# A DeltaNet and hardswish-MLP kernel on one core: the hand-written order of its first steps rewritten, the order of the loads with it

## The chip, the cores and the metric

The kernel runs on one core of a Trainium2 chip. The metric is the device time of one execution in microseconds (us). Before the change the median of three runs is 661.89 us (661.52 to 662.9). The engines are PE (TensorE, matmuls), DVE (VectorE), ACT (ScalarE), POOL (GpSimd) and SP (SyncE, which here only issues loads and stores). Each runs its own instructions in the order in which they were written; a semaphore holds an instruction back until what it reads is there.

## The reference

```
B, H, S, D = 4, 8, 768, 48
k_n = k / (norm(k, axis=-1) + 1e-6)
for t in range(S):                      # a state of D x D for each batch and head
    y[t] = q[t] @ state
    v_old = state^T k_n[t]
    state = state + beta[t] * outer(k_n[t], v[t] - v_old)
x = y as (3072, 384)
h = x @ w_in                            # 384 x 2048
out = (h * clip(h + 3, 0, 6) / 6) @ w_out   # 2048 x 384
```

The two weight matrices come as 64-bit floats, and the kernel converts them to FP32 itself.

## The kernel before

The recurrence over 768 tokens is cut into 24 chunks of 32 tokens (chunk t), all four batches side by side on 128 partitions. Chunk t needs a unit lower triangular 32x32 matrix per batch and head to be inverted. Chunk 0 is inverted alone by block products (`product`). Chunks 1 to 4 form group 1: their sixteen-row halves are solved together on DVE by `halves_of(1)`, and `join(t)` makes one inverse out of two halves. From chunk 5 on four chunks are solved together by `inverse(g)`. Two chunks give 256 tokens for the MLP (a block); `up` is its first matmul, `down` the second. The 16 weight pieces of 768 KB (eight of w_in, eight of w_out) are loaded raw and converted by ACT (four steps, L345) and DVE (three steps, L367, L372, L378).

For chunks 0 to 4, while the weights arrive, the order is not computed but written out: `ORDER` is a string of 782 words, `word*n` meaning n times. `do(word)` advances one generator by one step, and a step issues its instructions on one engine. So the string fixes the order on every engine, SP's loads included. After the string ends, a planner takes over whose code is the same in both kernels.

What the words issue, in the order of their steps (a chunk number follows the letter):

| word | steps |
|---|---|
| k, q, v | one load of 48 KB on SP (a chunk is four); L168, L180, L193 |
| w, W | one weight piece on SP, L320; W waits for the last PE instruction written before it |
| B | one load of beta, issued by ACT, L1383 |
| z | on DVE: zero pads; transpose of beta (L247); `eye`, `blocks`; `corner`; nothing; `parity` (nine small fills, L265 and L268) |
| s | on POOL: pads, and the state's zeros |
| n0, n1, n2, n4, n5 | key norms: square (ACT L396), sum (DVE L402), root (ACT L406), three small DVE steps, `inv` (DVE L420) |
| p | kb (POOL L499), transpose of keys (PE L513), copy KQ (ACT L521), transpose of queries (PE), copy KQ (ACT), products sc (PE L536), L and LB (DVE L547) |
| m, b | mask times beta (POOL L475); beta times kb (POOL L487) |
| x0 | `product(0)`: 16 steps; PE at L585, DVE L595 to L645, two ACT copies V at L613 and L632 |
| i1 | `halves_of(1)`: transpose A (DVE L458), 28 DVE steps, a fill, transpose X (DVE L462) |
| x1 to x4 | `join`: fill (POOL), transpose (DVE L683), PE L673, two DVE steps (L687, L691), PE L673, copy X (ACT L699) |
| h | `chain`: ks (PE L795, not for chunk 0), R (DVE L890, L898), pz (PE L816), copy Z (ACT L916), su (PE L927), state (DVE L945) |
| y | output: even (ACT L832), odd (DVE L808), py (PE L816), sum or copy (L850, L852), yt (PE L862), copy xT (ACT L866); chunk 0 has the last four only |
| a, c | the ACT steps (four a piece) and DVE steps (three a piece) of the weights |
| ua, ra, ga (ub, ...; u, ...) | `up` of one half block, one 128-wide part each: PE L983, ACT L990, DVE L993; u are the MLP's later units |

In the texts, `a2.1` is piece 2's second ACT step, `c6.0` piece 6's first DVE step, `W2` piece 2's load, `ga4` the fifth ga, and so on.

A part of `up` holds one of four PSUM banks until its ga has read it, so the fifth part behind it waits for that ga. `needs` in the code is a check on the written order only and issues nothing.

## Time and profile before

| | |
|---|---|
| median of three runs | 661.89 us (661.52 to 662.9) |
| profiled execution | 662.71 us; its span from first to last instruction 661.0 us, so 1.7 us lie around it |
| PE busy | 632.6 us of the span (96%) |
| DVE busy | 499.5 us (76%) |
| ACT busy | 263.2 us (40%) |
| POOL busy | 226.6 us (34%) |
| mean granted PE clock | 0.989 |
| DMA | 33.28 MB |

The page has a row for each engine in which a digit is the busy share of one fortieth of the span (16.5 us) in tenths. The view by windows gives busy microseconds of each engine in a stretch. The timeline lists the instructions of an engine with their start, duration and the idle time before them, with what ended it. The chain of waits follows the end of the run back from instruction to instruction.

### The profile page before, as it was taken

The page shows a single profiled execution, that of the slowest core. Times are in us where ns is not written, and L with a number is a line of the kernel's source. Part 1 is how long each engine was busy: PE and PEld are TensorE (multiplying, and loading weights), DVE is VectorE, ACT ScalarE, POOL GpSimd, SP SyncE. Part 2 cuts the span into 40 slices and gives each one's busy share as a digit, 9 for nine tenths or more (in the row PEclk, how much of TensorE's full clock was granted, in tenths as well). Part 3 has the DMA queues.
Part 4 walks back from the last instruction along what each step waited for, and adds up shares of the span by engine and source line. Part 5 has one row for each costly group of instructions (what it writes and reads, how often), then busy time and mean ns, then how long its engine had stood idle before and what let it go on. Part 6 is the DMA issues. An engine that isn't in the chain of part 4 may idle for free.

```text
span 661.0 us, 26631 instructions
## 1 busy us (share of the span) xinstructions
PE 632.6 (96%) x11640; PEld 568.8 (86%) x11640; DVE 499.5 (76%) x1164; ACT 263.2 (40%) x547; POOL 226.6 (34%) x352
## 2 busy tenths in 40 slices
PE   2768999999999999999999999999999999999997
PEld 2658987776689989999999999999999999999997
DVE  5899877798657988758988748979658998456354
ACT  4786578322232154154144244244244144153240
POOL 5531023003661354453254354164152241331330
PEclk9979999999999999999999999999999999999999
DMA  7888246212041030041030030030020020000101
GB/s 171 210 216 217 76 100 165 49 25 39 16 84 20 2 75 3 3 83 28 3 74 3 2 74 3 2 63 2 3 50 2 2 49 3 23 18 2 26 1 24
DMA packets 88692, 33.28 MB, mean 50 GB/s; under 512 B 80224, under 2 KB 83424, under 8 KB 88576
## 3 DMA queue, kind: packets, MB, share of 16 engines
q1 hardware_dynamic: 88224, 31.29, 21.5%
q8 instruction: 91, 1.49, 0.9%
q10 hardware_dynamic: 352, 0.30, 0.2%
q14 instruction: 25, 0.20, 0.1%
HBM read 26.84 MB, written 4.72 MB: 48 GB/s over the span
## 4 chain that ended last, share of the span: by engine, by line
PE 91%; DVE 3%; DMA 2%; ACT 2%; SPq 1%; issue 1%; ACTq 0%; DVEq 0%
PE po L1215 28%; PE ph L1055 27%; PE ph L983 9%; PE po L1151 6%; PE ks L795 4%; PE pz L816 3%; PE pt L513 3%; PE py L816 3%; PE su L927 3%; PE sc L536 3%; ACT spare L345 1%; PE yt L862 1%; DMA w_out<-in_moe_w_in_dram 1%; SPq L168 1%; PE pi L673 1%
## 5 line engine op out<-in xcount | busy, mean ns | idle before, releaser
L1055 PE MATMUL ph<-xT,w_in 128*128 128x128 f32 (+1 forms) x720 | 156.7, 321 | 0.2 <-issue 0.2
L1019 POOL TENSOR_TENSOR g<-g 128x256 f32<-128x256 f32 (+1 forms) x144 | 88.0, 612 | 105.5 <-ACT g L1069 99.9
L1055 PEld LDWEIGHTS ph<-xT,w_in 128*128 128x128 f32 x720 | 116.9, 191 | 6.7
L1215 PE MATMUL po<-w_out,g 128*128 128x192 f32 x640 | 110.6, 326 | 0.0
L1215 PEld LDWEIGHTS po<-w_out,g 128*128 128x128 f32 x640 | 104.6, 190 | 0.5
L1215 PE MATMUL po<-spare,g 128*128 128x192 f32 x480 | 86.7, 332 | 0.0
L1069 ACT ACTIVATE g<-ph 128x512 f32<-128x512 f32 x72 | 43.0, 597 | 107.5 <-PE ph L1055 107.5
L1215 PEld LDWEIGHTS po<-spare,g 128*128 128x128 f32 x480 | 77.2, 190 | 1.8
L983 PE MATMUL ph<-xT,w_in 128*128 128x128 f32 (+1 forms) x384 | 72.8, 339 | 1.5 <-ACT xT L866 0.6
L1225 POOL TENSOR_TENSOR o<-o,u 128x192 f32<-128x192 f32 x18 | 14.9, 828 | 163.5 <-ACT o L1222 76.1
L983 PEld LDWEIGHTS ph<-xT,w_in 128*128 128x128 f32 x384 | 60.2, 196 | 9.0 <-DVE g L993 0.9
L1082 DVE TENSOR_TENSOR g<-ph,g 128x256 f32<-128x256 f32 x72 | 30.2, 419 | 47.3 <-PE ph L1055 44.8
L748 DVE TENSOR_TENSOR pr<-A 128x30 f32<-128x30 f32 (+9 forms) x150 | 57.6, 384 | 3.3
L1201 DVE TENSOR_TENSOR g<-g 128x512 f32<-128x512 f32 x80 | 55.3, 712 | 3.6 <-PE po L1215 3.6
L1102 DVE SCALAR_TENSOR_TENSOR g<-o,g 128x512 f32<-128x512 f32 x72 | 52.5, 729 | 7.2 <-ACT o L1099 7.2
L753 DVE TENSOR_TENSOR A<-A,pr 128x30 f32<-128x30 f32 (+9 forms) x150 | 55.1, 367 | 3.3
L1055 PE MATMUL ph<-beta_tok,sums_in 128*128 128x128 f32 x288 | 55.9, 275 | 0.1
L1099 ACT ACTIVATE o<-g 128x512 f32<-128x512 f32 x72 | 45.4, 631 | 12.0 <-DVE g L1102 8.5
L345 ACT ACTIVATE spare<-spare 128x768 uint16<-128x768 uint16 (+1 forms) x56 | 47.3, 850 | 3.2 <-DMA kf<-in_k_dram 1.7
L499 POOL TENSOR_TENSOR kb<-kf,inv 128x384 f32<-128x384 f32 x24 | 21.7, 906 | 75.5 <-issue 42.6
L1222 ACT ACTIVATE o<-po 128x192 f32<-128x192 f32 x40 | 13.2, 330 | 83.2 <-PE po L1215 83.2
L1151 PE MATMUL po<-w_out,g 128*128 128x384 f32 x128 | 45.4, 490 | 0.0
(137 smaller groups left out, 1010.2 us busy)
## 6 DMA issues: line engine op xcount, KB each, us to landing
kf<-in_k_dram SPq DMA_DIRECT2D x96, 48.0 KB, 3.0
qb<-in_q_dram SPq DMA_DIRECT2D x96, 48.0 KB, 2.6
vf<-in_v_dram SPq DMA_DIRECT2D x96, 48.0 KB, 2.5
out_dram<-o SPq DMA_DIRECT2D x90, 48.0 KB, 1.6
spare<-in_moe_w_in_dram SPq DMA_DIRECT2D x4, 768.0 KB, 5.3
w_out<-in_moe_w_in_dram SPq DMA_DIRECT2D x4, 768.0 KB, 5.6
w_out<-in_moe_w_out_dram SPq DMA_DIRECT2D x4, 768.0 KB, 7.0
spare<-in_moe_w_out_dram SPq DMA_DIRECT2D x4, 768.0 KB, 4.9
```

Source lines behind the costliest of these rows:

```text
L345: nc.scalar.activation(out=z, in_=z if n else d.bitcast(I16)[:, :, :, 3], func=func, bias=value, scale=scale,)
L748: nc.vector.tensor_tensor(out=pv, in0=A[:, j + 1 :, j].unsqueeze(2).to_broadcast([n, w, j]), in1=A[:, j, 0:j].unsqueeze(1).to_broadcast([n ...
L753: nc.vector.tensor_tensor(out=A[:, j + 1 :, 0:j], in0=A[:, j + 1 :, 0:j], in1=pv, op=ALU.subtract)
L983: nc.tensor.matmul(ph[:, cols], lhsT=w_in[:, s, f * 128 : (f + 1) * 128], rhs=xT[:, s, cols], start=(s == 0), stop=(s == NKT - 1),)
L1019: nc.gpsimd.tensor_tensor(out=out, in0=a, in1=b, op=op)
L1055: nc.tensor.matmul(ph[:, n], lhsT=w, rhs=x, start=start, stop=stop, skip_group_check=True)
L1069: nc.scalar.activation(out=gt, in_=ph[:], func=ACTF.Copy)
L1099: nc.scalar.activation(out=r, in_=g, func=ACTF.Relu, bias=0.5, scale=1.0 / 6.0)
L1102: nc.vector.scalar_tensor_tensor(out=g, in0=r, scalar=1.0, in1=g, op0=ALU.min, op1=ALU.mult)
L1151: nc.tensor.matmul(pos[c][:], lhsT=gs[blk, f // 2][:, f % 2, c * P : (c + 1) * P], rhs=w_out[:, f, :], start=(f == 0), stop=(f == NFC - 1),)
L1201: nc.vector.tensor_tensor(out=A(f, *out, 4), in0=A(f, *a, 4), in1=A(f, *b, 4), op=op)
L1215: nc.tensor.matmul(ps[n][:], lhsT=A(f - f % 2, *a)[:, f % 2], rhs=b[:, f], start=(f == 0), stop=(f == HF - 1),)
```

## The change

The string holds the same 782 words, each as often as before, in another sequence. Its last 29 words stand as they did. Three checks on the order are added in the code, and none of them issues an instruction. On SP the first weight pieces now come after fewer key and query loads:

| piece | k and q loads ahead, before | after |
|---|---|---|
| W0 | 8 and 4 | 8 and 4 |
| W1 | 14 and 4 | 12 and 4 |
| W2 | 18 and 6 | 17 and 6 |
| W3 | 20 and 10 | 19 and 10 |
| W4 | 22 and 15 | 21 and 14 |
| W5 | 23 and 18 | 21 and 16 |
| W6 | 24 and 23 | 21 and 20 |
| W7 | 28 and 23 | 26 and 23 |

The start of the string, as far as the end of `halves_of(1)`, and the code:

```diff
 ORDER = """
-k*2 B*3 k*2 n0 k*2 z B s*2 n0*6 k*2 q*2 n1 q n1 q w k p0 z*3 k n1*2 k*2 n1*2 z p0*2 s k p0*3 a k a
-m0 a n2 m1 p0 x0*2 w q x0 n1 x0*3 c*2 n2 a k s p1*2 a s*2 k q s*2 x0 n2 k*2 c x0 n2 x0 w q a*4 q p1
-n2 k*2 a x0 m2 p1 c*2 p1 n2*3 b1 q b0 s p1 x0 q w x0 n2 q*2 c*3 x0 n4 k p1 k p2*2 x0*2 a*2 c a*2 q*3
-a*2 w v p3*2 q x0 q n4 p2*2 c p2 v c n4*2 a*3 z v n4 c a m3 v c p2 n4*2 q p2 k c b2 h0 c h0 w a*2 h0
-p4*2 a*2 m4 p3 q*4 h0 q k w p4*2 c*5 v*2 p3 k p3*3 k*2 p4*2 v*2 p4 m6 k a w a w i1*3 k i1*7 a i1*2 a
-i1*2 v i1*2 k b3 k y0 c y0*3 ua*2 ra*2 i1*3 w v ga v a*3 i1*2 ua i1 h1 i1 q w ua ra ua i1 ra*2 ga i1
-k ua a*2 ra ga i1 ga ua ra ua ra i1 ga i1*4 ua ga n5 x1*2 k x1 c a ra v a*2 ga x2 k*2 ga*2 ua*2 x1
...
+k*3 B*2 k n0*2 k n0 k*3 s n0*3 n1 q n1 q*2 n1 q w k*2 n0 p0 B*2 z k n1 z k m0 p0 n1 p0 n1 w s z p0*3
+a p0 x0*2 s x0*2 n1 x0 a c k p1 c s n2 x0 n2 q a s a p1 a q x0 s c k*2 s k n2*2 s x0 k x0 w q a n2*2
+a k a c s b1 x0 p1 n2 x0 z n2 a c q k q x0 p1 b0 c m1 q w p1*2 n2 x0 a k*2 m2 z c q c x0 q p2 p1 x0
+a*3 n4 a q c n4 a q a w p2 q c a n4 p2*2 v x0 p2 c n4 v n4 c q p3 b2 c a p3 v n4 a n4 p2 v a m3 c p3
+w h0 p2 p3 h0 a h0 p4 a q*2 c q a*2 p3 q h0 c*2 w p4 k c p4*2 c v q k p4 k p3*2 c m4 p4*2 y0 v k i1
+k a q m6 i1 v q w i1 q a i1 w i1 y0 a*2 i1*3 y0*2 ua*2 i1 v i1 a v*2 i1*3 c i1*3 b3 ua w k*2 ra a i1
+k ga ra a k i1 k i1 ga ra i1 ua i1 z ua i1 ga v ua ra n5 h1 i1 ga i1 a ra i1*3 a ua ra ua i1 w i1*2
+ga ra y1 k i1 ua x2 x1 ga x1 a k ga v x1 ra a n5 x1 k n5 ga k ra ua ga ua x1*2 ra h1 ga v ua ra a c
...
@@ settings
         pads(nc.vector, kbufs[0], qbufs[0])
+        past.add("first pads")
         yield
+        needs(*(("B", b) for b in range(B)))
         nc.vector.transpose(out=beta_tok[:].rearrange("p n h -> p (n h)"), in_=beta_hm)
@@ prep
+        needs("first pads")
         for j, src in enumerate((kb, qb)):
@@ chain
-        needs(("bkb", t))
+        needs(("bkb", t), ("state", t - 1))
         su = update() if t < N - 1 else []
@@ betas
             nc.scalar.dma_start(out=beta_hm[C * b : C * b + H, :], in_=beta[b])
+            past.add(("B", b))
             yield
```

Engine by engine, the moves that matter here read so:

| engine | before | after |
|---|---|---|
| ACT, beta's loads | three ahead of the first square, the fourth behind it | two ahead, two behind chunk 1's root |
| DVE, first norms | stt2 of chunk 0, inv, sum of chunk 1, transpose of beta | stt2 of chunk 0, sum of chunk 1, inv, pads, ..., transpose of beta |
| ACT, first copy V of x0 | a0.0, a0.1, a0.2, square, V | a0.0, V, a0.1, square, a0.2 |
| ACT, second copy V of x0 | a1.3, a2.0, KQ of chunk 1's keys, root, a2.1, KQ of its queries, V | root, a1.2, a1.3, KQ of chunk 1's keys, V, a2.0, KQ of its queries, a2.1 |
| PE, around x0's last products | sc of chunk 1, x0, kb transpose of chunk 2, x0 | sc of chunk 1, x0, x0, both transposes of chunk 2 |
| ACT, end of the first chunks | a5.3, KQ of chunk 3's keys, 4's keys, 3's and 4's queries, a6.0 to a6.3, y0 | KQ of chunk 3's keys, Z0, a5.0 to a5.3, KQ of 3's queries, 4's keys and queries, a6.0, a6.1, y0 |
| DVE, parity | between chunk 4's norm steps | between the 21st and the 22nd step of i1 |
| PE, first ups | three ua, ks of chunk 1, six ua, join | six ua, ks of chunk 1, three ua, join |
| SP, piece 12 (W) | behind the second ub | behind the tenth ub |

More of the change, by code (lines that the diff above doesn't have):

```diff
@@ L28 @@
-i1*2 v i1*2 k b3 k y0 c y0*3 ua*2 ra*2 i1*3 w v ga v a*3 i1*2 ua i1 h1 i1 q w ua ra ua i1 ra*2 ga i1
-k ua a*2 ra ga i1 ga ua ra ua ra i1 ga i1*4 ua ga n5 x1*2 k x1 c a ra v a*2 ga x2 k*2 ga*2 ua*2 x1
-ra*2 x1*2 ua h1*2 n5 k ga c ra ga*2 h1 c y1*2 ua ra w ga ua ra x2 n5 ga y1*2 ua ra ga h1 v*3 n5*2 k
-y1*2 ua a ra x2 ub*2 a n5 rb*2 h1 x3 ga c*2 v W a h2 y2 gb ub rb gb x2 gb ub*2 n5*2 b4 rb n5 x2*2 h2
-gb rb gb m5 a n5*2 y2 ub rb gb v c q*2 v q*5 n5 ub n5 rb gb h2 c h2 q ub y2 h2 y2 rb ub p5 b5 rb
@@ L33 @@
-gb*2 a*2 x3 p5 ub y2*2 k p5*2 h2 rb h3 p5 gb h3 ub*2 q rb gb rb gb ub a x3 p6 v c x4 x3 rb gb ub p7
-rb gb y3 c*2 v c p7*2 y3 v p7*2 b6 x3 q x3 ub p6 h3 a p6 c p5*2 rb gb k m7 w p6 h3 u p6 k*2 q*3 a*2
-y3 a p6 c y3 v y3*2 u n9 v k q a c a c*2 u*2 ru gu w k a*2 c a*2 x4 c*2 ru p7 a gu k u a*2 p7 p6 m8
-u*3 a k u*2 k h3 w ru*2 a*2 gu*2 x4 c*2 x4 k c*2 a p8 k a*2 u ru k h3 u*2 h4 ru a b8 gu k gu y4 p8*3
-u h4 k*2 c q k*9 q u p8*2 x4 k ru k*2 gu k c n9 q u q*2 p8 k*2 b7 n9*2 i2 u x4 q i2*2 q ub ru gu u
@@ L38 @@
-rb gb i2*2 h4*2 u*2 i2 ru i2*6 y4 i2 gu i2*7 u i2 ru gu i2 u*3 ru i2*4 gu ru i2*2 v i2 c gu u*3 a u
-ru c i2 u*2 i2 gu i2*3 q i2*5 y4 h4 n9 i2 e*2 n9*2 i2*4 q i2 y4 e n9 u ru i2*3 u i2 ru*2 gu h4 u n9
-i2*2 u i2 e i2*6 y4 u k n9*3 u gu i2 y4 n9 i2 p9 q i2*2 gu
+k*3 B*2 k n0*2 k n0 k*3 s n0*3 n1 q n1 q*2 n1 q w k*2 n0 p0 B*2 z k n1 z k m0 p0 n1 p0 n1 w s z p0*3
+a p0 x0*2 s x0*2 n1 x0 a c k p1 c s n2 x0 n2 q a s a p1 a q x0 s c k*2 s k n2*2 s x0 k x0 w q a n2*2
+a k a c s b1 x0 p1 n2 x0 z n2 a c q k q x0 p1 b0 c m1 q w p1*2 n2 x0 a k*2 m2 z c q c x0 q p2 p1 x0
@@ new lines @@
+ra ga c ua h1 c h1 y1 ua ra a ga y1 k ra h1 n5 y1 x2 ga ua ra ga y1*2 ua ra q x2 v ub ga rb ub c a
+rb c h1 ga h2 n5 w x2 ub k gb rb gb q n5 h2 gb ub q v rb x3 x2 v ub x2 rb ub b4 n5 gb rb gb v n5 ub
+n5 gb c q h2 n5 y2 rb q h2 ub q y2 n5 c n5*2 ub y2 h2 y2 gb y2 rb ub rb a q gb a*2 rb p5 gb b5 a W k
+x3 gb p5 ub y2 h2 v rb ub v p5 v a h3 p5 q a gb k p7 x3 k rb ub m5 h3 gb y3 k ub p5 p6 v x3 rb c p7
+gb v rb gb ub b6 c y3 c p7 x3 p7 x3 p6 p7 c h3 a p6 v p5*2 h3 p7 rb w a p6 m7 q u p6 y3 k c y3 c x4
@@ new lines @@
+k p6 a k y3 u gb y3 q u a*3 k q a c u c u ru k gu k ru n9 c*2 u p6 p7 a*2 gu w a k u*2 w a p8 ru*2 c
+a x4 c k m8 a q k gu k q c u a u c x4 gu k h3 c k x4 u h3 a k ru q u gu ru b8 gu p8 a k p8 q c h4 p8
+h4 a y4 u*3 k*2 a q p8*2 k a k n9 x4 ru k*3 gu k u c q*2 p8 n9*2 i2 u x4 q i2 q i2 k q ub ru gu u rb
+gb i2*2 h4*2 u*2 i2 ru c i2*2 b7 i2*3 y4 i2 gu i2*7 u i2 ru gu i2 u*3 k ru i2*5 gu ru i2*2 v i2 c gu
+u*3 a u ru c i2 u*2 i2 gu i2*3 q i2*5 y4 h4 n9 i2 e*2 n9*2 i2*4 q i2 y4 e n9 u ru i2*3 u i2 ru*2 gu
@@ L41 @@
+h4 u k*2 n9 i2*2 u i2 e i2*6 y4 u k n9*3 u gu i2 y4 n9 i2 p9 q i2*2 gu
 """
```

## The prediction

> **What bounds the kernel now.** I read the page's slices first, then the view by windows, then the chain of waits, then the timelines of ACT and DVE.

> ```profile
> PE   2768999999999999999999999999999999999997
> DVE  5899877798657988758988748979658998456354
> ACT  4786578322232154154144244244244144153240
> PEclk9979999999999999999999999999999999999999
> ```

> PE is full from the fifth slice (66 us) to the end, and what follows the string is the same code. So the change is worth what it moves the moment from which PE is full, plus what it does to PE's few gaps behind that. The windows cut that start into stages (columns: PE, PEld, DVE, ACT, POOL busy us, granted clock, DMA share, GB/s):

> ```profile
> 31.00:36.00 5.00, 4.27 (x156) 3.55 (x160) 4.24 (x17) 2.48 (x5) 1.96 (x2) 0.60 0.88 217
> 36.00:40.00 4.00, 2.71 (x126) 2.44 (x115) 3.83 (x8) 3.90 (x6) 2.57 (x3) 0.50 0.63 116
> 40.00:46.70 6.70, 4.94 (x204) 4.23 (x202) 6.47 (x13) 6.43 (x11) 0.83 (x1) 0.84 0.86 185
> 46.70:59.70 13.00, 10.26 (x121) 9.29 (x121) 12.21 (x40) 8.33 (x18) 2.26 (x5) 0.87 0.98 280
> 59.70:71.00 11.30, 10.20 (x367) 9.15 (x368) 9.74 (x27) 6.40 (x17) 2.14 (x4) 1.00 0.35 95
> 71.00:83.00 12.00, 12.00 (x442) 11.22 (x442) 9.94 (x28) 7.08 (x19) 1.83 (x2) 1.00 0.40 101
> ```

> From 36 to 59.7 us DVE is the full engine (3.83 of 4.00, 6.47 of 6.70, 12.21 of 13.00, where its steps on group 1 follow each other without a gap longer than 0.1). From 71 PE is. The handover is in the chain (start, length, what):

> ```profile
> 46.75 1.88 DVE A L458
> ...
> 57.67 1.99 DVE X L462
> 59.78 0.37 DVE sums_in L683
> 60.19 0.73 PE pi L673 x54
> ```

> DVE transposes group 1's matrices (L458, at 46.67 in the timeline), solves, transposes back (L462), and the first join's transpose (L683, 59.69) lets PE start its product at 60.19. By then PE has done the same nine `ua` and one ks in both orders, with 0.57 and 0.92 us of idle time just ahead. So PE has room there, and **the start of L683 is the moment to be forecast**.

> Where DVE still waits, ahead of 46.67, the timelines say (start, length, what, idle before and its end). ACT:

> ```profile
> 15.18 0.51 ACT L396 ACTIVATE sq<-kf 128x384 f32<-128x384 f32 x1
> 15.59 0.36 ACT L613 ACTIVATE sums_in<-pi 128x256 f32<-128x256 f32 x1
> ...
> 22.46 0.93 ACT L345 ACTIVATE spare<-w_out 128x768 uint16<-128x768 int16 x1 [0.42 <-DMA w_out<-in_moe_w_in_dram]
> ...
> 25.09 0.38 ACT L632 ACTIVATE sums_in<-pi 128x256 f32<-128x256 f32 x1
> ```

> and DVE:

> ```profile
> 7.11 0.20 DVE L420 RECIPROCAL inv<-nt 128x8 f32<-128x8 f32 x1
> 7.36 0.55 DVE L402 TENSOR_REDUCE ss<-sq 128x8 f32<-128x384 f32 x1
> ...
> 25.50 0.45 DVE L634 STREAM_TRANSPOSE sums_in<-pi 128x256 f32<-128x256 f32 x1 [0.82 <-ACT sums_in L632]
> ...
> 40.28 1.01 DVE L945 TENSOR_TENSOR state<-state,su 128x384 f32<-128x384 f32 x2
> ```

> **The change, part by part.** All 782 words stay, so no engine gains or loses work; only waits change. I walk DVE's new sequence with the durations of the old rows.

> 1. *First norms.* `inv` of chunk 0 (7.11) goes behind chunk 1's sum (7.36), into the place that the transpose of beta had at 7.83. POOL's kb started 0.29 behind `inv`, at 7.40, so now at 8.12, and with it its transposes, KQ and sc: the first L moves from 12.25 to 12.97, a loss of 0.72.

> 2. *Beta.* Its last load started at 5.10, and the DMA view shows that queue's last packets between 6.5 and 7.0, so it takes at most 1.9. Now two loads follow chunk 1's root (7.94 to 8.15), at about 0.4 each: the last starts at 8.55 and has landed by 10.45. Transpose 0.97 and POOL's mask 1.19 make 12.6, ahead of 12.97. Hidden by 0.35; without that cover it costs what it overruns.

> 3. *First V of x0.* It ran at 15.59, behind two ACT steps of W0 and a square, though PE was done at 14.95. Now only a0.0 is ahead of it, which waits for W0 (SP's issue 7.49, landed 12.56, same place in SP's queue) and ends at 13.5. PE ends at 14.95 + 0.72 = 15.67, V starts at 15.7 and DVE's transpose at 16.1 instead of 15.99. Of 0.72 only 0.1 is left.

> 4. *Second V of x0.* It ran at 25.09, behind a2.0 (22.46, which had waited for W2), a KQ, a root and a2.1; DVE stood still for 0.82 and, for that root, 0.53. Now it stands ahead of all of piece 2. PE's product, at 22.19 to 23.27, gets the 0.1; ACT reaches V at about 23.85 (a1.2, a1.3 and one KQ behind the root at 21.4), DVE is free at 24.45 and transposes there: 1.05 early. One wait is new: PE's next product of x0 stands behind sc of chunk 1, whose second KQ is now behind a2.0, so it ends at 28.7 and DVE goes on at 28.75 against 30.09; one c step that stood ahead follows now. At c3.1 DVE is 0.96 early (32.45 against 33.41).

> 5. *The weight pieces.* W1 to W6 lose one to five loads ahead of them, at 0.45 to 0.49 each on SP; W5 went out at 31.93 and by the same sum goes out near 28.5. Before, ACT waits once for a piece at 0.42 (22.46) and once for PE at 2.49 (33.88). I value earlier pieces by themselves at nothing: ACT is full from 24 us in the new order (24 steps of 0.85 and the KQ until 43), and no piece is late for it. If they gave all they could, it would be that 0.42. W12 goes out later, behind the tenth `ub` (82 us) instead of at 73.3; its first reader on ACT is at 99, and a piece lands in 4.5 to 8.4.

> 6. *State of chunk 0.* DVE's step at 40.28 follows su (38.43 to 39.73). New: sc of chunk 2 at 34.4 (34.53), pz 1.50, Z at 37.4, where ACT ends a4.3 and a KQ (37.90), su at 38.0 to 39.3. DVE, free at 38.3, waits for it a microsecond and goes on at 39.35: still 0.93 early. Then three steps of piece 5 and c6.0, L of chunk 3, c6.1, L of chunk 4 (KQ's end at 43.1, sc at 44.2, both in time): 6.4 us as before, so L458 at 45.75 against 46.67, **0.92 early**. This also counts that parity (34.75 to 35.27, 0.52) has left this stretch.

> 7. *Parity* now lies between two steps of the solve: 0.5 more from L458 to L683, otherwise the same 13.02 (28 steps, both transposes, c6.2, ga0 to ga5). `ua` starts near 47.8 instead of 48.99 and PE's room ahead of the join grows; no gain comes of that, as the join still stands behind nine `ua`. L683: 59.69 - 0.92 + 0.5 = 59.27, **0.42 early**.

> 8. *Behind it*, from 60.19 to 70.99 (the second join's product), PE idles 0.31 and 0.30. The new sequence sends su of chunk 1 ahead of a `ua`, and puts the sum of chunk 1's output (DVE, due 9.2 us behind L683) just ahead of PE's need. I count 0.55 back; nothing or the full 0.61 are the ends.

> Sum: 0.42 + 0.55 = 0.97, so about **1.0 us less**: 661.7 for the profiled execution (662.71, of which 1.7 lies outside the span), and 660.9 from the median, 0.8 below it. The largest doubts are steps 4 and 6, waits that no row shows: without any of step 4's gain the sum is +0.1, without step 6's new wait -1.5 (below). POOL's masks and kb products move beside other c steps, which take 0.95 alone and up to 1.47 beside POOL: one or two more or fewer is 0.5 either way.

> **The rivals.**

> *A warmer PE* (-1.6 to -3). From 32 to 42 us the granted clock is 0.50, and sc takes 1.18 instead of 0.86, pz 1.50 instead of 0.88, su 1.30 instead of 0.89. In the new order x0's last product and three transposes stand together near 30 to 33. At full clock su ends 1.3 earlier, step 6's wait goes, and then KQ on ACT is the limit: L458 at 45.2, the sum 1.55, 660.3; with early pieces 0.4 more. For it: PE's gap of 1.96 at 29 us shrinks. Against: PE was busy only 1.01 of 2 us from 28 on, and the new order fills that little better.
> [...]

> *Late beta* (slower). Two beta loads now go out while W0 is in flight. In the stretch from 10 to 20 us a q load of 48 KB takes a median 4.9 from issue to landing. At that price beta lands at 13.45, its mask is done at 15.6, and the first L comes at 15.6 instead of 12.97: 2.65 on the whole chain, **663.5**. It decides from 10.8 (0.35 of cover), turns the sum's sign at 11.8 and reaches a measurable loss at 13.1. Against it: before 10 us loads took 2.2 to 2.5, and beta goes on ACT's own queue.
> [...]

> *The order does nothing* (661.5 to 663.5). DVE and ACT are full from 24 us on, so waits that go in one place come back in the next; parity's 0.5 and the first 0.72 stay.

> **How the numbers follow.** Forecast, 0.60, own range 659.7 to 662.2 (-2.2 to +0.3 by the doubts above). Warmer PE 0.18. Late beta 0.13. Nothing 0.09. A measurement of this kernel tells about 0.2%, 1.3 us, from no change: faster is below 660.6, slower above 663.2. The forecast lies 0.22 in faster, 0.38 in same; warmer PE wholly in faster; late beta in slower; nothing 0.05 in same, 0.04 in slower. Faster 0.40, same 0.43, slower 0.17. The range leaves out the far ends of warmer PE and late beta: 659.0 to 663.4.

> **What would show it.** L547's first row at 12.97 (step 1; later means beta); L613 at 15.7; L634 at 24.5; the state step at 39.4 with a wait for su; L458 at 45.8; L683 at 59.3; PE without a gap from there to 71. Wrong I would be if L458 doesn't move, if a `ga` between the solve's steps waits for ACT or a late W7, or if PE shows new gaps behind 71 us.

## The result and the profile after

| | before | after |
|---|---|---|
| median | 662.09 us (4 runs, 661.52 to 662.9) | 671.28 us (4 runs, 670.27 to 672.8) |
| ratio | 1 | 1.014, 95% interval 1.0117 to 1.0162 |
| profiled execution | 662.71, span 661.0 | 670.27, span 668.5 |

The new order is 9.2 us slower; the forecast was 1.0 faster. (The ratios below leave out one disturbed execution, that of g3's profile, from which places are read and not times.) The page's slices of after:

```profile
PE   1658998999999999999999999999999999999997
DVE  3878885799748888858988848988748988457354
ACT  2876486522232234234244234234234143143240
PEclk9987999999999999999999999999999999999999
```

PE's string lies below that of before in the first three slices and the seventh, is level with it in between, and behind the seventh both are 9 up to the last. So the loss lies in the first 120 us, where the windows place it (columns as before: PE, PEld, DVE, ACT, POOL, clock, DMA share, GB/s):

```profile
31.00:36.00 5.00, 3.26 (x108) 2.63 (x100) 4.10 (x9) 4.94 (x9) 3.20 (x4) 1.00 0.71 160
36.00:40.00 4.00, 1.88 (x100) 1.56 (x104) 3.74 (x10) 3.31 (x5) 1.28 (x1) 0.87 1.12 300
40.00:46.70 6.70, 5.43 (x220) 4.41 (x216) 3.69 (x7) 5.74 (x9) 1.85 (x3) 0.82 0.74 126
46.70:59.70 13.00, 7.98 (x129) 7.06 (x121) 10.99 (x29) 6.71 (x12) 2.27 (x5) 0.61 0.95 277
59.70:71.00 11.30, 10.34 (x315) 9.61 (x314) 10.36 (x41) 7.18 (x19) 1.00 (x2) 1.00 0.13 24
71.00:83.00 12.00, 10.81 (x372) 9.98 (x373) 9.37 (x25) 5.15 (x14) 0.00 (x0) 1.00 0.40 98
100.00:120.00 20.00, 17.58 (x324) 12.49 (x325) 12.84 (x24) 13.62 (x22) 6.56 (x8) 1.00 0.64 166
```

The last stretch in before:

```profile
100.00:120.00 20.00, 19.86 (x323) 14.73 (x323) 14.48 (x28) 15.59 (x24) 5.08 (x5) 1.00 0.65 151
```

Two things are new. From 40 to 46.7 us DVE is no longer full (3.69 of 6.70, before 6.47). And PE, which had not one idle moment from 71 to 83 us before, has 1.19 there and 2.42 from 100 to 120 (before 0.14). DVE's timeline shows where it falls behind (start, length, what, idle before and its end):

```profile
13.29 0.98 DVE L250 STREAM_TRANSPOSE beta_tok<-spare 128x768 f32<-128x768 f32 x1 [5.03 <-DMA kf<-in_k_dram]
...
15.61 0.42 DVE L551 TENSOR_TENSOR X<-sc,sums_in 128x256 f32<-128x256 f32 x1 [0.58 <-POOL sums_in L478]
...
43.97 1.02 DVE L949 TENSOR_TENSOR state<-state,su 128x384 f32<-128x384 f32 x2 [2.87 <-PE su L931]
```

(Lines in after are 1 to 4 higher.) The first loss is beta: transposed at 13.29 instead of 7.83, and the first L follows at 15.61, against 12.97 forecast. DVE's row puts the wait down to a load of keys; the two late loads of beta are what it reads, issued by ACT at 7.82 to 8.45, and in the DMA view their queue q10 moves nothing from 8.5 to 10.5 and is done by 12.0. The trace's semaphore events tell of the two landings only at 12.66 and 13.17. The second loss is in the chain of waits:

```profile
46.29 0.71 PE sc L540 x44
47.00 3.32 issue
50.32 0.64 PE sc L540 x18
51.06 0.42 DVE L L551
51.48 0.33 DVE LB L551
51.81 1.89 DVE A L461
...
63.12 1.96 DVE X L465
65.21 0.37 DVE sums_in L687
65.62 0.73 PE pi L677 x54
...
72.56 0.46 PE su L931 x23
73.03 1.19 issue
74.21 0.69 PE su L931 x39
```

In the middle of the 64 equal matmuls of one step PE stands still for 3.32 us. "Issue" means that it waits for nothing that the profile shows. Such **stops** (those of 0.15 us or more) sum to 1.10 us of PE's timeline in before (0.31 the longest) and to 9.98 in after. The account: the join's product starts at 65.62 instead of 60.19, 5.43 of the 7.5 by which the span grew; of the other 2.07, stops behind it are 2.69 more, and 0.62 was won elsewhere. The account takes a stop behind the join at its length, and one ahead of it only at what it delays the join by.

### The profile page after: what moved, and what is told of

The parts are those of the page before. It is cut to its first block, busy times and chain, and to the rows that moved or that the text cites. A ratio compares the mean times of both kernels' runs of the same rounds, so it can differ in the third digit from the quotient of the medians.

```text
span 668.5 us, 26626 instructions
## 1 busy us (share of the span) xinstructions
PE 632.1 (95%) x11640; PEld 568.4 (85%) x11640; DVE 496.6 (74%) x1164; ACT 261.9 (39%) x547; POOL 225.9 (34%) x352
## 3 DMA queue, kind: packets, MB, share of 16 engines
q1 hardware_dynamic: 88224, 31.29, 21.4%
## 4 chain that ended last, share of the span: by engine, by line
PE 90%; issue 3%; DVE 3%; ACT 2%; SPq 0%; DMA 0%; POOL 0%; ACTq 0%; POOLq 0%; DVEq 0%
PE po L1219 28%; PE ph L1059 27%; PE ph L987 9%; PE po L1155 6%; PE ks L799 4%; PE pz L820 3%; PE py L820 3%; PE su L931 3%; PE pt L517 3%; PE sc L540 3%; ACT spare L348 2%; PE yt L866 1%; PE pi L677 1%; DVE A L728 1%; ACT KQ L525 0%
## 5 line engine op out<-in xcount | busy, mean ns | idle before, releaser
L1229 POOL TENSOR_TENSOR o<-o,u 128x192 f32<-128x192 f32 x18 | 13.5, 751 | 164.8 <-ACT o L1226 76.1
L1155 PE MATMUL po<-w_out,g 128*128 128x384 f32 x128 | 45.2, 489 | 0.0
```

The costliest lines, as they stand in the source:

```text
L1155: nc.tensor.matmul(pos[c][:], lhsT=gs[blk, f // 2][:, f % 2, c * P : (c + 1) * P], rhs=w_out[:, f, :], start=(f == 0), stop=(f == NFC - 1),)
```

## The experiments

Two theories: (a) beta's lateness; (b) PE's instructions: that they arrive in blocks, and that PE uses these up faster than they come. Rival to (b): the order itself, through its data waits or its loads. Ratios are to before on the same chip, with 95% intervals. A word order's diff is given as the move in it.

**Beta early in the new order, late in the old one.**

```diff
 e1_beta_early (after)          -k*3 B*2 k ... p0 B*2 z k
                                +k*3 B*4 k ... p0 z k
 e2_beta_late (before)          -k*2 B*3 k*2 n0 k*2 z B s*2 ... p0 z*3 k n1*2
                                +k*2 B*2 k*2 n0 k*2 z s*2 ... p0 n1 B*2 z*3 k n1
```

> The changed kernel with all four beta loads ahead of the first square on ACT; nothing else moved. Late-beta theory (the two late beta loads delay DVE's transpose of beta to 13.29 us, L to 15.61, and hold W1 on SP until 12.68, and all else follows): first L at about 13.0, W1 out near 9.5, L458 near 46 to 47 instead of 51.73, time 660 to 663 us. Rival, the order itself (the new sequences of PE, DVE and ACT are slower even with beta in time): first L at 13.0 all the same, but 666 us or more. Rival, the loads (W2 can't leave before W1 has landed, and PE's instruction loads come among the weight pieces): W2 still out later than 15.42, PE still stops in the middle of sc or su for over 1 us in all ahead of 60 us, 664 us or more.

> The kernel before with two of the four beta loads moved behind chunk 1's root on ACT, as the change has it; nothing else moved. Late-beta theory: transpose of beta at about 13.3 instead of 7.83, first L at about 15.6 instead of 12.25, 3.4 us late; part of it is taken up by waits that DVE had anyway (1.4 ahead of the first V's reader, 0.5 and 0.8 further on), so 663.5 to 666 us. Rival, the order itself or the loads: the late first L is absorbed, 661.5 to 663 us.

Measured: e1 668.81 us, 1.0063 (1.0036 to 1.0090); e2 668.99, 1.0082 (1.0057 to 1.0106); both lie above what the theory of late beta alone gave. Beta is worth 0.8% from either side, 5 us, where the first L moves by only 2.76 (15.61 to 12.85) and 3.76 (12.25 to 16.01). And 0.6% stays when beta is early. DVE's timeline of e1:

```profile
12.85 0.42 DVE L551 TENSOR_TENSOR X<-sc,sums_in 128x256 f32<-128x256 f32 x1 [2.88 <-PE sc L540]
...
16.03 0.45 DVE L619 STREAM_TRANSPOSE sums_in<-pi 128x256 f32<-128x256 f32 x1 [0.86 <-ACT sums_in L617]
...
24.39 0.44 DVE L638 STREAM_TRANSPOSE sums_in<-pi 128x256 f32<-128x256 f32 x1
...
29.53 0.45 DVE L643 STREAM_TRANSPOSE sums_in<-pi 128x256 f32<-128x256 f32 x1 [1.76 <-PE pi L589]
...
42.59 1.02 DVE L949 TENSOR_TENSOR state<-state,su 128x384 f32<-128x384 f32 x2 [2.89 <-PE su L931]
...
51.46 1.94 DVE L461 STREAM_TRANSPOSE A<-L 128x1024 f32<-128x1024 f32 x1
```

Up to 24.39 us this is the forecast's walk to about a tenth (12.97, 16.1, 24.45). From there on it waits for PE, and L461 comes 5.7 later than forecast. PE's stops by then: 0.45 at 26.5, 1.79 at 32.4, 0.90 at 37.7, 1.94 at 42.2, 4.64 at 50.1.

**The loads' order alone.** e3 gives e1 the loads of before as far as W6; e4 gives before the loads of after (beta early in both).

```diff
 e3_loads_before (e1, SP only)  k, q, v and w from the start to W6 in the sequence of before
 e4_loads_after (before, SP only)  k, q, v and w in the sequence of after
```

> The changed kernel with all four beta loads early and SP's loads in the old sequence up to W6; PE, DVE, ACT and POOL as changed. If the loads' order costs: faster than the same kernel with the new loads by 1 us or more, 661 to 662.5. If the new sequences of the compute engines cost by themselves: 665 us or more here too. Late-beta theory: both within 1.3 us of each other, 660 to 663.

> The kernel before with SP's loads in the new sequence, beta early as before; PE, DVE, ACT and POOL as before. If the loads' order costs (W2 waits for W1 to land, pieces come together with PE's instruction loads): 664 us or more. Late-beta theory and the theory of the compute engines' order: within 1.3 us of the kernel before, 660.8 to 663.4.

Measured: e3 1.0080 (1.0053 to 1.0106), no better than e1; e4 1.0039 (1.0009 to 1.0069). e4's ten executions lie in two groups, four at 662.7 to 663.5 and six at 666.2 to 670.8. Its profile is of the first group (662.91): it has two stops that before lacks, 1.31 at 36.6 and 1.17 at 41.4, and they cost nothing there that could be told; what the other six lost is not shown. The order of the loads is not what holds e1.

**Light pieces.** Both orders with W6 to W15 loaded only in part (16 KB each in place of 768 KB; what the kernel computes with them is then not the reference's).

```diff
+        n, m = (1, 32) if i >= 6 else src.bitcast(U32).shape[1:]
-            out=raws[i].rearrange("p s f z -> p s (f z)"), in_=src.bitcast(U32)
+            out=raws[i].rearrange("p s f z -> p s (f z)")[:, 0:n, 0:m],
+            in_=src.bitcast(U32)[:, 0:n, 0:m],
```

> The kernel before with pieces 6 to 15 loaded only in part, the control for the run above. Both theories: no stop of PE over 0.4 us, as before, 660 to 662.5 us. If the light pieces speed it up by more than 1.5 us, the pieces cost the kernel before something too, by their data and not by PE's instructions.

> The changed kernel with beta early, and weight pieces 6 to 15 loaded only in part (32 words of each partition's first row instead of 768 KB; the output is not the reference's). All instructions stay, in the same order. Code-loading theory (PE stops in the middle of its blocks of 64 small matmuls because its next 16 KB of instructions come slowly while weight pieces are in flight): the stops ahead of 35 us stay (0.45 and 1.79 in the run with full pieces), those at 37.7, 42.2 and 50.1 us (0.90, 1.94, 4.64) and at 73 to 105 us shrink to a few tenths each, L458 comes near 46 instead of 51.46, time 659 to 663 us. Rival, the order itself: PE, DVE and ACT keep the long waits, 665 us or more.

Measured: f0 0.9980 (0.9963 to 0.9996), f1 665.84 us, 1.0038 (1.0021 to 1.0055). f1 is a miss: the theory of supply gave 659 to 663, the rival 665 or more (whether the order itself is the slower one is tested at four places below). (f0 has one stop of 0.47 at 39.2, where none over 0.4 was expected.) Stops fall from 12.6 to 6.7 us in e1's order, which fits traffic that lengthens them, but the distance of the two orders stays, 0.6%.

**The count of matmuls.** The stops seemed to lie close to a multiple of 128 matmuls apart (126 to 128 from one to the next in e1). Queue q8 (kind "instruction") on the page of before:

```profile
q8 instruction: 91, 1.49, 0.9%
```

```diff
     with tc.manual_schedule():
+        lead = psM.tile([128, 512], FP32, name="lead", tag="pm3")
+        for i in range(64):          # 128 matmuls; range(32): 64; and so on
+            nc.tensor.matmul(lead[0:32, 0:32], lhsT=ident[0:32, 0:32], rhs=ident[0:32, 0:32], ...)
```

> The kernel before with 64 extra matmuls of 32x32 on PE ahead of everything, in the first 8 us in which PE has nothing to do; they write a PSUM bank that is overwritten later. The order of the rest is unchanged. Code-loading theory: the places at which PE needs its next 16 KB of instructions (every 128 matmuls) all move 64 matmuls forward, so stops of PE come at other places, and the time moves by 1 us or more, up to 670. Rival (order and data alone set the time): 661.5 to 662.6 us, no new stop.

> The changed kernel with beta early and the same 64 extra matmuls ahead of everything. Code-loading theory: the stops that lay at the third last matmul of sc of chunk 2, the eighth last of su of chunk 0 and the eighteenth last of sc of chunk 4 lie 64 matmuls earlier in PE's sequence, their lengths are others, and the time differs from that of the kernel without the extra matmuls by 1 us or more either way. Rival, the order itself: the time is the same within 1 us.

Each of the 64 calls came out as two matmuls (x128 in g1's rows), so this became a shift by a whole block, where 64 were meant. Measured: g1 1.0012 (0.9997 to 1.0027), g3 1.0084 (1.0060 to 1.0109), near before and e1. Stops of PE in e1, then in g3 (xN: what is left of the block of small matmuls behind the stop):

```profile
42.23 0.33 PE L931 MATMUL su<-R,sums_in 32*64 32x48 f32 x8 [1.94 <-issue]
50.05 0.63 PE L540 MATMUL sc<-KQ 64*32 64x64 f32 x18 [4.64 <-issue]
...
104.91 0.78 PE L540 MATMUL sc<-KQ 64*32 64x64 f32 x55 [0.70 <-issue]
```

```profile
42.58 0.46 PE L931 MATMUL su<-R,sums_in 32*64 32x48 f32 x8 [2.83 <-issue]
47.79 0.41 PE L540 MATMUL sc<-KQ 64*32 64x64 f32 x18 [1.09 <-issue]
...
111.20 0.78 PE L540 MATMUL sc<-KQ 64*32 64x64 f32 x55 [0.97 <-issue]
```

The same matmul each time, after 128 more. The places stay, the lengths do not: g1 stops for 2.12 at 41.8, at a place where before had no stop. Counted from PE's first matmul, added ones included, 16 of the 20 profiles of this case have a stop of 0.2 us or more at matmul 729, 730 or 731. Half a block was the next test, with two that bunch small matmuls or spread them.

```diff
 p1_early_spread (e1, PE only)    su of chunk 1 from behind y1 to behind the next ua; sc of chunk 7 from behind that of 5 to behind the second u
 p2_before_bunched (before, PE only)  su of chunk 1 to directly behind py; sc of chunk 7 to directly behind that of 5
```

> After with the two late beta loads early (as e1), and two blocks of PE's order set apart: the su block of chunk 1 behind the next ua, so that it no longer follows py directly, and the sc block of chunk 7 behind u2, so that it no longer follows that of chunk 5 directly. Nothing else is moved. Theory of instruction supply: PE stops in bunched small matmuls because they use up its instructions faster than queue q8 brings them; the stops near 73 us (0.84 in e1) and near 100 and 105 us (1.38 and 0.70) vanish or fall below 0.5 in sum, and the time is 2 to 3 us below e1's 668.8: ratio to before 1.001 to 1.004. Rival, the order itself or its data waits: the stops may move, the ratio stays at 1.005 to 1.009.

> Before with only these two bunchings put in: the su block of chunk 1 directly behind py, and the sc block of chunk 7 directly behind that of chunk 5. Theory of instruction supply: stops of PE that wait for nothing shown appear near 70 us (about 1 us) and near 97 to 102 us (1 to 2 us), and the time rises by 1 to 3 us: ratio 1.0015 to 1.0045. Rival, the small matmuls are supplied as fast as the rest and the loss of after is one of data waits: no stop above 0.4 us there, ratio 0.999 to 1.001.

> Before with 64 more matmuls on PE ahead of its first transposes (work that is thrown away, half of the 128 at which the stops recur); done before the first load it waits for. Theory of instruction supply: every place at which PE could stop moves by 64 matmuls, so that the stops of before (0.31 near 65, 69 and 100 us) are gone or elsewhere, and others appear by where the new places fall; the time moves by up to 2 us either way, ratio 0.997 to 1.003. Rival, stops that belong to certain instructions and not to a count: same places, ratio 0.999 to 1.001.

> After with the two late beta loads early, and the same 64 more matmuls on PE. Theory of instruction supply: the stops at 26.5, 32.4, 37.7, 42.2, 50.1, 73.6, 100.6 and 104.9 us of e1 appear 64 matmuls earlier in PE's order, in the middle between them; where these fall in large matmuls they shrink; ratio 1.003 to 1.009. Rival, stops that belong to certain instructions: places as in e1, ratio 1.006 as e1.

p2, 1.0039 (1.0016 to 1.0061), is as the theory of supply had it: stops of 1.03, 1.70 and 0.68 at 69.4, 97.5 and 101.8. (One of 0.80 at 40.8 lies ahead of both moved blocks.) PE's timeline there:

```profile
67.97 0.45 PE L930 MATMUL su<-R,bkb 32*64 32x48 f32 x24
69.44 0.69 PE L930 MATMUL su<-R,bkb 32*64 32x48 f32 x40 [1.03 <-issue]
```

p1, 1.0059 (1.0035 to 1.0082), is a miss: the stops near 73 and 105 went down, but 2.00 appeared at 93.8 in a join. To spread two blocks did not help here, as the place of the next packet fell into a third. g5: 1.0099 (1.0073 to 1.0126). **g4: 1.0155 (1.0127 to 1.0182)**. Before, with 64 useless matmuls ahead of all its work, loses 10 us, as much as the whole change; I had the kind right and the size five times too small. PE's timeline of g4:

```profile
40.68 0.36 PE L816 MATMUL pz<-vf,X 32*32 32x48 f32 x2 [2.72 <-issue]
53.89 0.54 PE L816 MATMUL py<-R,LB 32*32 32x48 f32 x16 [4.24 <-issue]
```

Its page has one packet of q8 more, 92.

**Both orders at four places.** If the place decides, an order has to be judged by more than one.

```diff
-        for i in range(32):
+        for i in range(16):   # g6 (before), g8 (e1), g10 (after): 32 matmuls
+        for i in range(48):   # g7 (before), g9 (e1): 96 matmuls;  g11: after with range(32)
```

> Before with 32 more matmuls on PE ahead of its first transposes (thrown away; a quarter of the 128 at which the stops recur). With no more it takes 1.000, with 64 more 1.0155. Theory of supply, by which the time depends on where in PE's order the places at every 128 matmuls fall: every stop lies 32 matmuls earlier than in before, and the ratio lies between 1.000 and 1.016, not at one of the two for a reason of its own. Rival, the 1.0155 came from the added work itself (3.6 us on PE at the start, ahead of its first wait): half of that work costs half, 1.007 to 1.009, and the 96 of the next kernel 1.023.

> Before with 96 more matmuls on PE at the start. Theory of supply: stops 96 matmuls earlier than in before (32 later than with no more); ratio between 1.000 and 1.016. Rival, the added work itself: above 1.0155, near 1.023, though 128 more gave 1.0012, which speaks against it already.

> After with the two late beta loads early (e1), and 32 more matmuls on PE. Question of these four: what the order costs over the four starting places, not at one. If the order is worth nothing by itself and before had the best of its four places by luck, the mean of e1 over 0, 32, 64 and 96 lies within 1.5 us of that of before over the same four (two known of each: before 1.000 and 1.0155, e1 1.0063 and 1.0099), and one of the four of e1 may lie at 1.002 or below. If the new order is the worse in its supply or its waits, e1 lies above before in the mean by 2 us or more.

> As the kernel ahead with 96 more matmuls in place of 32: ratio between 1.000 and 1.012 by either theory; the mean over four decides.

> After itself (late beta loads) with 32 more matmuls on PE, thrown away, done ahead of the first load that it waits for. With beta early the same start gave 1.0126. If the late beta costs its 2.8 us at the first factor wherever PE's stops fall, this gives 1.015 to 1.018; if PE's supply hides it (an engine that is held by supply doesn't notice a later beta), 1.011 to 1.0135; if lateness adds as much as at the first place (0.0077), 1.020.

> After itself (late beta loads) with 64 more matmuls on PE. With beta early the same start gave 1.0099. Full price of the late beta at the first factor, 2.8 us: 1.0125 to 1.0155; hidden by supply: 1.008 to 1.011; as at the first place: 1.0176. Its stops (0.42 at 33.4, 1.66 at 38.9, 0.79 at 43.6, 3.32 at 50.3, 1.19 at 74.2, 1.08 and 1.52 past 100) lie 64 matmuls earlier by the theory of supply.

Ratio, and in brackets the sum of PE's stops in the profiled run, us (the profiled run of e1 with 96 took 677.73, 5.3 above its median):

| matmuls added | before | e1 (after, beta early) | after |
|---|---|---|---|
| 0 | 1.0000 (1.1) | 1.0063 (12.6) | 1.0140 (10.0) |
| 32 | 1.0152, 1.0110 to 1.0194 (10.2) | 1.0126, 1.0098 to 1.0154 (7.4) | 1.0146, 1.0096 to 1.0197 (8.2) |
| 64 | 1.0155, 1.0127 to 1.0182 (12.5) | 1.0099, 1.0073 to 1.0126 (10.4) | 1.0115, 1.0073 to 1.0156 (9.4) |
| 96 | 1.0092, 1.0064 to 1.0119 (6.1) | 1.0138, 1.0121 to 1.0155 (16.5) | |
| 128 | 1.0012, 0.9997 to 1.0027 (2.1) | 1.0084, 1.0060 to 1.0109 | |
| mean of 0 to 96 | 1.0100 | 1.0107 | |

The added work itself is not the cause: 128 of them cost 0.1%, 32 cost 1.5%. The means of the two orders lie 0.0007 apart, 0.45 us, with the intervals combined from -0.8 to +1.7: over these four places the new order is neither better nor worse that could be told. (The intervals carry the noise of the runs, not the choice of four places out of 128.) Before has one place of four that suits it, and it starts there, by luck or by tuning, which the record does not say. (The fastest place of e1, 1.0063, is not among those below 1.002 that I thought possible, and g5 and g9 lie above the 1.009 and 1.012 that I had set as their ends.) The sum of stops is not the loss: e1 has 12.6 us of them at 1.0063 and 7.4 at 1.0126. Nor does the place alone fix the time: the eight executions of g7 run from 664.4 to 673.2, the eleven of before beside them from 661.8 to 665.0. The stops of g5 and of g11, the same PE order with beta early and late, fall on the same matmuls:

```profile
48.03 0.69 PE L820 MATMUL py<-R,LB 32*32 32x48 f32 x18 [2.52 <-issue]
...
98.59 1.34 PE L540 MATMUL sc<-KQ 64*32 64x64 f32 x109 [0.80 <-issue]
104.00 0.80 PE L820 MATMUL py<-R,LB 32*32 32x48 f32 x55 [1.95 <-issue]
```

```profile
48.98 0.68 PE L820 MATMUL py<-R,LB 32*32 32x48 f32 x18 [1.07 <-issue]
...
98.78 1.34 PE L540 MATMUL sc<-KQ 64*32 64x64 f32 x109 [1.45 <-issue]
103.92 0.80 PE L820 MATMUL py<-R,LB 32*32 32x48 f32 x55 [1.68 <-issue]
```

Late beta costs 0.0077, 0.0020 and 0.0016 at the three places, each give or take 0.004 to 0.006: in the mean 2.5 us, give or take 1.8. One by one, g10 and g11 fall between the cases that I had set apart.

**Could it be the granted clock?** It was half speed (0.50 in the windows) in changing stretches of the first 60 us. The windows of e2 and of g1:

```profile
24.00:36.00 12.00, 8.37 (x301) 6.72 (x303) 9.08 (x18) 9.39 (x15) 4.74 (x6) 1.00 0.88 199
36.00:48.00 12.00, 8.13 (x234) 6.84 (x224) 9.15 (x27) 8.44 (x13) 4.27 (x5) 1.00 0.94 197
```

```profile
24.00:36.00 12.00, 8.79 (x288) 7.33 (x292) 9.98 (x28) 9.10 (x15) 5.09 (x5) 0.50 0.79 171
36.00:48.00 12.00, 7.92 (x304) 7.00 (x300) 10.10 (x18) 9.60 (x15) 3.40 (x3) 0.53 0.86 202
```

e2 has the full clock and takes 1.0082; g1 has half of it and takes 1.0012. In the first 60 us the clock does not decide it. Further on it adds to some of the stops. In g6 PE stops for 2.42 until 105.2, and then:

```profile
100.00:106.40 6.40, 3.98 (x139) 2.74 (x138) 2.97 (x6) 3.33 (x5) 1.50 (x2) 1.00 0.76 186
106.40:109.80 3.40, 3.40 (x9) 2.14 (x8) 1.52 (x2) 2.18 (x4) 0.00 (x0) 0.50 0.84 259
```

PE is busy there throughout at half speed, an estimated loss of 1.7 us. From 66 to 650 us the 20 profiles hold ten such stretches (eight of 3.4 us, one of 6.8 and one of 10.2), and each begins within 1.5 us of the end of a stop, the shortest of 1.58 (g8). Nine other stops of 1.5 to 2.1 were followed by none, and in after and e1 there is no such stretch.

## Why the prediction was wrong

Two steps failed, and one assumption under three others.

- **Step 2, beta hidden with 0.35 to spare: failed.** The last load took not 1.9 us but 5.0 (issued at 8.13, landed at 13.17), and the first L came at 15.61, as the late-beta rival had it (15.6). That rival's price of 2.65 is the 2.76 by which e1's first L is earlier, and the mean over three places agrees (2.5). At the place of the kernel as it is, it is 5.0, and there the stops that follow are others too. The rival's chance of 0.13 was far too low: it rested on 2.2 to 2.5 us for loads ahead of 10 us, and the row of 4.9 under W0 was the nearer one. Late beta also held back W1, which SP issued at 12.68 (9.38 in e1); SP's waits of after:

```profile
SPq L323 <- DMA spare<-in_beta_dram: 3.4, 1, 3.4
```

 ACT's own queue did not keep beta from W0: beside it (issued at 6.75, landed at 12.55) q10's packets started 2.4 to 3.6 us after the start of the last issue, against 1.0 to 1.7 in before, where they ran ahead of W0.
- **Steps 4, 6 and 8 assumed that PE stops only for data: failed.** In e1, where beta is early, steps 1, 3 and the first half of 4 came true (12.85, 16.03, 24.39). What follows did not: state at 42.59 for 39.35, L461 at 51.46 for 45.75, behind 9.7 us of stops ahead of 60 us. Step 8's two gaps of 0.31 and 0.30 did go, but I had read them as waits to be saved. They were stops of the same kind (both are marked "issue", the one sign in the profile of before), and 3.79 us of others came behind the join, the new gaps behind 71 us that the prediction had named as a sign of being wrong.
- **Step 5, earlier pieces worth nothing:** true in the new order (e3 is no different from e1); in the old one the new loads cost 0.4%, and no profile shows where.
- **Step 7, parity:** 13.40 from L461 to L687, 13.52 forecast. Right.
- **The warmer PE:** the clock did rise (1.00 from 31 to 36, where before had 0.60) and nothing came of it; e2, at full clock there too, is slower as well. That a shorter gap of PE would keep the clock up was an estimate and is not shown: from 66 us on the clock fell at stops of 1.58 (g8) to 3.26 (g9), and at nine others of 1.5 to 2.1 it did not.

What is shown: stops lie where the count of PE's instructions puts them, every 128 matmuls or close to it, and to shift the count moves the time by up to 1.5%. No row names the wait, but the times of q8's packets in the traces do. The longest stop of e1 ends at 50.05; q8 in the DMA view of its 42 to 50.1, then of 47.4 to 47.5:

```profile
q8 instruction: 1, 0.02, 1.0%
```

```profile
q8 instruction: 1, 0.02, 79.1%
```

So one packet came in those 8 us; it started at 47.4, took 1.27 (79.1% of 0.1 us on 16 engines), was done at 48.7, and PE went on 1.34 later. It is so everywhere: each of the 120 stops of 0.2 us or more in the 20 profiles ends 1.15 to 1.80 us behind the end of a q8 packet (the ten of before and after 1.22 to 1.64), where packets come over 3 us apart. The reverse holds as well. Take 1.45 us behind a packet's end as the moment from which PE can go on. At the first 20 places of each profile (400; those between stops are interpolated) PE has a stop of 0.2 us or more where that moment lies 0.2 or more behind its arrival, and none elsewhere, in 375; in the other 25 the moment lies at most 0.55 behind it. So the stops are waits for q8's packets.

When a packet starts shows too. With few exceptions it started only after PE had passed the place ahead, 128 matmuls earlier: in the median 2.3 us after it for places passed from 15 to 56 us, where the weight pieces come, and 1.1 from 60 to 96. The packet of e1's longest stop started 5.2 us after the place ahead (42.23). Why that one took 5.2 and the next 2.3 stays open.

A block of 64 of the small matmuls takes 0.86 to 1.50 us in before (sc, pz, su), and one such place cost PE up to 4.64 us (e1), a kernel 10 us (g4).

## What to carry to other kernels

Where PE runs many small matmuls (here 64 in 0.86 to 1.50 us), look for "issue" in the middle of a block of equal matmuls, and for the end of an instruction packet just ahead of PE's going on: this kernel moved by 1.5% when 32 or 64 matmuls shifted PE's count (g6, g4), and one comparison of its two orders measured their places as much as the orders (e1 against before: 0.0063 at the places that they had, 0.0007 in the mean of four). Shift both by a few counts (some useless matmuls at the start) ahead of a verdict. To set large matmuls between the blocks of small ones is the obvious cure, but the one trial of it here (p1, 1.0059 against e1's 1.0063) gained nothing that could be told. A load that many steps wait for is priced by the row of loads issued beside the same big transfer, not by the quiet rows ahead of it (here 4.9 against 2.2 to 2.5 us, and beta's took 5.0).

## What the runs showed that I had not expected

- 64 matmuls of 3.6 us in all, run while PE had nothing else to do, cost 10 us (g4), and 128 cost 0.8 (g1).
- In 20 profiles no two of PE's stops of 0.21 us or more ended less than 3.86 us apart (g7); from 25 to 55 us, under the weight pieces, the least was 4.28 (p1), and e1's from 42.23 to 50.05 was 7.82.
- The granted clock of the first 60 us differs from kernel to kernel (half speed from 24 to 45 in g1, at no time from 12 to 60 in e2), and between these two the slower kernel is the one with the full clock.
